# A gated mix of a 2-D spectral filter and a gated feed-forward: token pairs in the row layout, a sum of block products begun in PSUM, operand sums in place, half of the tiles by way of DRAM

## The chip, the cores and the metric

The kernel runs on one core of a Trainium2 chip. The metric is the device time of one execution in microseconds (us). A profiled execution of the kernel before gives the trace that is read here; three more give the times.

## The reference

Two branches are computed from the same x (2048 tokens by 576 features, float32) and mixed with a gate for each token:

```python
def _A_ref(x, w_r, w_i):
    X = jnp.fft.rfft2(x, axes=(-2, -1))
    X = X * (w_r + 1j * w_i)
    return jnp.fft.irfft2(X, s=(S, D), axes=(-2, -1))

def _B_ref(x, w_gate, w_up, w_down):
    g = jnp.einsum("bsd,df->bsf", x, w_gate)
    u = jnp.einsum("bsd,df->bsf", x, w_up)
    return jnp.einsum("bsf,fd->bsd", _gelu(g) * u, w_down)

g = _sigmoid((x * gate_w).sum(-1, keepdims=True))
return g * a + (1 - g) * b
```

The hidden size of the feed-forward is 4608, so branch B is three large matrix products; branch A is a Fourier transform over tokens and features, a product with a filter, and the way back.

## The kernel before

**The feed-forward** fills TensorE (PE). Each float32 operand is split into a high and a low part, so that a product of 128x512 takes three matmuls (high·high, high·low, low·high) plus tails. `PLAN` lists 36 steps in order: `"c"*2 + "s"*10 + "c"*11 + "s"*13`, the first half of the tokens in the first 18 and the second half in the others. A `c` step (`conv`) computes its products plainly. An `s` step (`products`) computes a 2x2 block product with seven products in place of eight: a11, a12, s2, s1, s3, s4, a22, numbered n = 0 to 6, each in two halves s = 0 and 1 of seven matmuls (`seven`, L1041 to L1044). The `s` operands (s1 to s4 and the splits of a11, a12, a22, in the tiles sx, gu2, xhi, xlo) are made once for each half of the tokens by `operands(p)`, from blocks that `load_xs` brings into xraw, tmp and misc. After each block, `down` multiplies the hidden tiles hb and hx with w_down (L835, pieces of twelve matmuls of 288 columns); ScalarE (ACT) scales the result into stg (L860), and GpSimd (POOL) adds it to yd in DRAM.

**PSUM** holds three pairs of banks that matter here: pgu, pone and pdn. In an `s` step the result of n = 0 stands in the banks of one pair and n = 1 in the other. ACT copies the first into gl (L214, `gl<-pgu` or `gl<-pone`), VectorE (DVE) adds the second to it (L1077), and `finish` takes gelu (L1068, ACT), the product with the other half (L1062, DVE), the rounding to the high part (L214, `hb<-gl`) and the low part (L1065, DVE). n = 2, 3, 4, 5, 6 go on in the same banks and in xraw.

**The spectral branch** (`spectral`) runs beside this on DVE and ACT, with some matmuls in `columns`. Its row transform of 576 points works on a tile `rows` of 128 x 5120 in which eight tokens are interleaved: element k of token t stands at 8k + t. It goes by a stage of nine (`forward_rows`) and radix-4 stages of width 8, 32 and 128 (`stage`, `_butterfly` L87) with `small_twiddles` (L444) and `large_twiddles` (L456). `into_tiles` and `into_rows` move between `rows` and `til`, in which each token has 290 elements in a row, with `moved` (L500): an ACT copy and a DVE product with a sign (L507) for each token, 289 elements at a time. `gate_sum` (L683) sums x·gate_w for a token. `columns` is the transform over tokens.

**The order.** Every engine takes its instructions in the order of the program, and the program's order is written by the kernel itself: PE pieces call `gap()` (L656), which pulls work from the generator `spectral` as long as `credit` is positive. Each PE piece adds its length to the credit (`tick`), each yielded DVE operation takes its own off, and the credit is cut at 1.2 us (L663). `at(n, …)` puts work n gaps later, and `seq`/`due` issue the steps of a hidden tile. `starts` are the two first steps of the runs of `s` (PLAN places 2 and 23); there the list `downs`, which says how many down pieces follow each of the seven products, differs from the other steps, because fewer hidden tiles are waiting.

## Time and profile before

| what | value |
|---|---|
| median of three runs | 1376.58 us (1374.06, 1376.58, 1377.76) |
| the profiled execution | 1374.25 us |
| its span, first to last instruction | 1372.5 us |
| mean granted clock of TensorE | 0.958 of full speed |
| DMA | 227.42 MB, 166 GB/s in the mean |

The span is what the trace covers; the execution's own time is 1.75 us longer. In the tables a line is given as `L1077`, then the engine, the operation, and `out<-in` by the names of the program. An idle time is put down to the instruction or DMA that released the engine last. A matmul's entry lasts longer than its spacing, because matmuls are pipelined: the next one starts before the entry of the last ends.

### The profile page before, as it was taken

The page shows a single profiled execution, that of the slowest core. Times are in us where ns is not written, and L with a number is a line of the kernel's source. Part 1 is how long each engine was busy: PE and PEld are TensorE (multiplying, and loading weights), DVE is VectorE, ACT ScalarE, POOL GpSimd, SP SyncE. Part 2 cuts the span into 40 slices and gives each one's busy share as a digit, 9 for nine tenths or more (in the row PEclk, how much of TensorE's full clock was granted, in tenths as well). Part 3 has the DMA queues.
Part 4 walks back from the last instruction along what each step waited for, and adds up shares of the span by engine and source line. Part 5 has one row for each costly group of instructions (what it writes and reads, how often), then busy time and mean ns, then how long its engine had stood idle before and what let it go on. Part 6 is the DMA issues. An engine that isn't in the chain of part 4 may idle for free.

```text
span 1372.5 us, 20070 instructions
## 1 busy us (share of the span) xinstructions
PE 1344.1 (98%) x7364; PEld 1186.9 (86%) x7364; DVE 1142.8 (83%) x1605; ACT 846.9 (62%) x1444; POOL 263.2 (19%) x322
## 2 busy tenths in 40 slices
PE   9998999999999999999999999889999999999998
PEld 7887888888889888889888988767888888888888
DVE  7689999989999768867786587689989779989854
ACT  5585676666674455465665544676676776676682
POOL 0011122221122222122210111211222232222231
PEclk9999999999999999999999999989999999999999
DMA  9465776696667877799987657744666797667797
GB/s 332 163 128 146 148 142 131 130 272 129 126 110 147 195 139 148 181 236 236 265 233 222 132 109 206 173 98 103 130 132 129 134 266 131 135 116 137 138 220 181
DMA packets 102770, 227.42 MB, mean 166 GB/s; under 512 B 12432, under 2 KB 22672, under 8 KB 101776
## 3 DMA queue, kind: packets, MB, share of 16 engines
q0 software_dynamic: 44928, 90.98, 44.1%
q1 hardware_dynamic: 57744, 135.17, 29.7%
q8 instruction: 57, 0.93, 0.3%
q14 instruction: 41, 0.34, 0.1%
HBM read 121.70 MB, written 97.26 MB: 160 GB/s over the span
## 4 chain that ended last, share of the span: by engine, by line
PE 85%; DVE 6%; ACT 4%; DMA 2%; issue 2%; SPq 0%; DVEq 0%; ACTq 0%
PE pdn L835 30%; PE pgu L1041 5%; PE pgu L1043 5%; PE pgu L1042 5%; PE pone L1041 5%; PE pgu L760 5%; PE pgu L762 5%; PE pgu L761 4%; PE pone L1043 4%; PE pone L1042 4%; PE pgu L1044 2%; PE pone L1044 2%; PE pone L760 2%; PE pone L762 2%; PE pone L761 2%
## 5 line engine op out<-in xcount | busy, mean ns | idle before, releaser
L848 POOL DMA_DIRECT2D yd<-stg x264 | 228.9, 868 | 994.2 <-ACT stg L860 861.2
L860 ACT ACTIVATE stg<-pdn,omg 128x576 f32<-128x576 f32 x276 | 203.9, 739 | 278.7 <-PE pdn L835 274.1
L835 PE MATMUL pdn<-dn,hb 128*128 128x288 f32 x2556 | 371.2, 295 | 2.5 <-DVE hb L1065 1.3
L835 PEld LDWEIGHTS pdn<-dn,hb 128*128 128x128 f32 x2556 | 357.8, 189 | 14.3 <-DVE hb L1065 1.8
L214 ACT ACTIVATE gu<-wq 64x256 fp32r<-64x256 f32 (+4 forms) x353 | 228.5, 666 | 101.7 <-DVE gu L1006 90.9
L1006 DVE TENSOR_TENSOR gu<-wq,gu 128x768 fp32r<-128x768 f32 x161 | 153.5, 953 | 18.9 <-ACT gu L214 18.5
L835 PE MATMUL pdn<-dn,hx 128*128 128x288 f32 x876 | 134.2, 295 | 0.2 <-DVE wq L899 0.2
L835 PEld LDWEIGHTS pdn<-dn,hx 128*128 128x128 f32 x876 | 124.9, 189 | 4.1 <-DVE wq L899 0.5
L760 PE MATMUL pgu<-xhi,gu 128*128 128x512 f32 x300 | 117.9, 393 | 0.0
L762 PE MATMUL pgu<-xlo,gu 128*128 128x512 f32 x300 | 117.8, 393 | 0.0
L761 PE MATMUL pgu<-xhi,gu 128*128 128x512 f32 x300 | 117.7, 392 | 0.0
L1023 DVE TENSOR_TENSOR wq<-wq 128x768 f32<-128x768 f32 x92 | 87.7, 953 | 7.9 <-ACT gu L214 7.9
L214 ACT ACTIVATE hb<-gl 128x512 fp32r<-128x512 f32 x66 | 41.4, 627 | 51.4 <-DVE gl L817 51.4
L762 PEld LDWEIGHTS pgu<-xlo,gu 128*128 128x128 f32 x300 | 56.6, 189 | 12.3
L760 PEld LDWEIGHTS pgu<-xhi,gu 128*128 128x128 f32 x300 | 56.8, 189 | 9.9
L761 PEld LDWEIGHTS pgu<-xhi,gu 128*128 128x128 f32 x300 | 56.7, 189 | 9.9
L1044 PE MATMUL pgu<-sx,gu 128*128 128x512 f32 x138 | 54.5, 395 | 6.6 <-ACT sx L214 6.6
L739 DVE TENSOR_TENSOR dn<-wq,dn 128x576 fp32r<-128x576 f32 x72 | 54.2, 753 | 5.0 <-ACT dn L214 5.0
L1041 PE MATMUL pgu<-xhi,gu 128*128 128x512 f32 x140 | 55.6, 397 | 2.5 <-DVE xraw L1077 2.4
L1041 PE MATMUL pgu<-sx,gu 128*128 128x512 f32 x140 | 55.7, 398 | 1.9 <-ACT gl L214 1.9
L1041 PE MATMUL pone<-xhi,gu 128*128 128x512 f32 x136 | 53.5, 394 | 3.7 <-DVE xraw L1077 3.7
L1043 PE MATMUL pgu<-sx,gu 128*128 128x512 f32 x140 | 55.2, 395 | 0.0
(243 smaller groups left out, 2871.2 us busy)
## 6 DMA issues: line engine op xcount, KB each, us to landing
yd<-stg POOLq DMA_DIRECT2D x264, 288.0 KB, 4.9
wq<-ws SPq DMA_DIRECT2D x92, 384.0 KB, 4.2
wq<-wd SPq DMA_DIRECT2D x72, 288.0 KB, 4.6
wq<-wgu SPq DMA_DIRECT2D x24, 640.0 KB, 5.8
colm<-col POOLq DMA_DIRECT2D x32, 256.0 KB, 6.3
tmp<-wf SPq DMA_DIRECT2D x16, 290.0 KB, 5.1
hx<-til SPq DMA_DIRECT2D x64, 72.5 KB, 5.0
til<-hx SPq DMA_DIRECT2D x64, 72.5 KB, 3.7
```

The costliest lines, as they stand in the source:

```text
L214: act.activation(o, i, AF.Copy)
L760: pe.matmul(ps, w[:, 0, k, c], xhi[tb][:, k], start=k == 0, stop=False)
L761: pe.matmul(ps, w[:, 1, k, c], xhi[tb][:, k], start=False, stop=False)
L762: pe.matmul(ps, w[:, 0, k, c], xlo[tb][:, k], start=False, stop=False)
L835: pe.matmul(ps[half], h[:, l, c], d[:, k, half * HD:(half + 1) * HD], start=part == 0 and n == 0, stop=part == 1 and n == 2)
L848: pl.dma_start(yd[u], o, accum_op=ALU.add)
L860: put(u, lambda o: act.activation(o.rearrange("p (c k) -> p c k", c=2), v[:, :, 0:HD], AF.Copy, scale=omg[:, u:u + 1]), i == 0)
L1006: vec.tensor_tensor(o, x.rearrange("p (c k) -> p c k", c=3), f(w[:, 256:1024]).rearrange("p (c k) -> p c k", c=3), ALU.subtract)
L1041: pe.matmul(ps, hi, xh[:, t], start=start and t == 0, stop=False, skip_group_check=True)
L1042: pe.matmul(ps, lo, xh[:, t], start=False, stop=False, skip_group_check=True)
L1043: pe.matmul(ps, hi, xl[:, t], start=False, stop=False, skip_group_check=True)
L1044: pe.matmul(ps, tl, xt, start=False, stop=stop, skip_group_check=True)
```

## The change

Five things are done together.

1. **Token pairs.** `rows` interleaves two tokens where it interleaved eight, in four groups. The radix-4 stages have the widths 2, 8 and 32, the small twiddles work on runs of 2, `moved` handles a pair of tokens in one instruction, and gates and output rows read every second element. The copies to and from the layout of `xn` follow (its load is now two DMAs).
2. **The first sum in PSUM.** In an `s` step ACT copies the result of n = 0 not into gl but into the other pair of banks (`copy(ps[1][s], v)`), and n = 1 accumulates onto it. The two DVE additions into gl go; gelu reads the bank (L1232 after) and so does the product (L1167 after). n = 1 now has to wait for the copy. `downs` changes in both forms.
3. **Operand sums in place.** `operands` forms s1 to s4 in the loaded blocks, with all three parts loaded earlier, its ACT copies handed out two at a step, and only s4 left for the last `c` step. The second set is loaded right behind `columns`.
4. **Half the tiles through DRAM.** The second eight tokens' tiles go to `bw` straight from `til`, and `fetched_rows` reads them back in pieces; before, they were moved into `rows` first and went to DRAM in that form. `fw` is written and read in quarters.
5. **Placing.** The credit is cut at 2.0 us in `columns` (`COLCAP`); the reload of x for the second half goes at other gaps; the weight slots (`early`, `where`) of the last `s` step before a `c` follow its place.

```diff
+COLCAP = 2.0
...
+        bw = dram.tile([P, 8 * SW], F32, name="bw", tag="bw")
...
+        def token_rows(rows, t):
+            return rows.rearrange("p (c g k t) -> p g t c k", c=2, g=4, t=2)[:, t // 2, t % 2]
...
-            v = rows.rearrange("p (b d e t) -> p b d e t", d=4, e=4, t=8)
-            tmps = [tmp[:, 320 * i:320 * (i + 1)].rearrange("p (b t) -> p b t", t=8) for i in range(4)]
-            tmps = [(x, x[:, 0:20], x[:, 20:40]) for x in tmps]
+            v = rows.rearrange("p (b d e t) -> p b d e t", d=4, e=4, t=2)
+            tmps = [tmp[:, 320 * i:320 * (i + 1)].rearrange("p (b t) -> p b t", t=2) for i in range(4)]
+            tmps = [(x, x[:, 0:80], x[:, 80:160]) for x in tmps]
...
+            yield from stage(rows, 2, TAKEN, -1)
+            yield from small_twiddles(rows, TAKEN, -1)
             yield from stage(rows, 8, TAKEN, -1)
-            yield from small_twiddles(rows, TAKEN, -1)
+            yield from large_twiddles(rows, TAKEN, -1)
             yield from stage(rows, 32, TAKEN, -1)
-            yield from large_twiddles(rows, TAKEN, -1)
-            yield from stage(rows, 128, TAKEN, -1)
...
         def moved(at):
 
+            s2 = sgn[:, None, :].to_broadcast([P, 2, KF])
             yield None
-            for t in range(8):
+            for g in range(4):
                 for c in range(2):
-                    o, i = at(t, c)
+                    o, i = at(slice(2 * g, 2 * g + 2), g, c)
                     if c:
-                        vec.tensor_tensor(o, i, sgn, ALU.mult)
-                        yield 0.66
+                        vec.tensor_tensor(o, i, s2, ALU.mult)
+                        yield 0.69
                     else:
                         copy(o, i)
-                yield None
+                if g % 2:
+                    yield None
...
+        def fetched_rows():
+
+            rows = rows_tile()
+            R = row_view(rows)
+            pl.memset(rows.rearrange("p (c k) -> p c k", c=8)[:, :, 2 * KF:], 0.0)
+            s2 = sgn[:, None, :].to_broadcast([P, 2, KF])
+            for b in range(2):
+                for i, x in enumerate(spots_of[b]):
+                    g, c = divmod(i, 2)
+                    o, x = R[:, 2 * b + g, c, :, 0:KF], x[:, :, 0:KF]
+                    if c:
+                        vec.tensor_tensor(o, x, s2, ALU.mult)
+                        yield 0.69
+                    else:
+                        copy(o, x)
+                if b == 0:
+                    yield None
+                    fetch(1)
+                    for _ in range(5):
+                        yield None
+            box[0] = rows
...
+            yield from beside(first_tiles(1))
             yield from into_tiles(0, rows)
             yield from first_tiles(0)
             cols[0] = True
             yield from columns()
             cols[0] = False
+            load_xs(1)
             yield from last_tiles()
-            load_xs(1, 0)
-            load_xs(1, 1)
-            yield from into_rows(1)
-            nc.sync.dma_start(bw, box[0])
             yield None
+            for i in range(4):
+                c = slice(2 * SW * i, 2 * SW * (i + 1))
+                nc.sync.dma_start(bw[:, c], til[0][:, 8 * SW:][:, c])
+                yield None
             yield from into_rows(0)
             yield from operands(1)
             yield from until(3)
+            fetch(0)
             yield from inverse_rows(0)
-            box[0] = rows_tile()
-            nc.sync.dma_start(box[0], bw)
-            for _ in range(5):
-                yield None
+            yield from fetched_rows()
             yield from inverse_rows(1)
...
+            credit[0] = min(credit[0], COLCAP if cols[0] else 1.2)
...
+            def sums(i):
+                a11, a12, a21, a22 = parts_of[i]
+                for o, x, z, op in ((a22, a21, a22, ALU.add), (a21, a11, a21, ALU.subtract),
+                                    (a11, a22, a11, ALU.subtract), (a12, a12, a11, ALU.subtract)):
                     vec.tensor_tensor(o, x, z, op)
-                    yield 0.72
-                sums = (("s1", m), ("s2", a11), ("s3", a21), ("s4", a12))
-                yield None
-                if i == 2:
-                    yield from tails_of([(ops[n][2], x) for n, x in sums])
-                else:
-                    for n, x in sums:
-                        copy(ops[n][0][:, i], x)
+                    yield 0.61
...
+                for n in raw:
+                    high(n, 2)
+                yield from sums(0)
+                for n in most:
+                    high(n, 0)
+                yield from sums(1)
+                for n in raw:
+                    low(n, 2)
+                    quarter(n)
+                    yield 0.61
+                for n in most:
+                    high(n, 1)
+                for n in most:
+                    low(n, 0)
+                    yield 0.61
+                while acts:
                     yield None
+                yield from sums(2)
+                for n in most:
+                    high(n, 2)
+                for n in most:
+                    low(n, 1)
+                    yield 0.61
+                while acts or current[0] < starts[p] - 1:
                     yield None
-                    for n, x in sums:
-                        vec.tensor_tensor(ops[n][1][:, i], x, f(ops[n][0][:, i]), ALU.subtract)
-                        yield 0.61
-                if i == 0:
-                    load_xs(p, 2)
+                for i in range(3):
+                    high("s4", i)
+                for n in most:
+                    low(n, 2)
+                    quarter(n)
+                    yield 0.61
+                while acts:
+                    yield None
...
+                if name == "c11":
+                    seq((name, q), (1, mult), (2, lambda: copy(h[:, 0], g)), (4, low))
+                elif done:
...
-            downs = (1, 1, 1, 1, 0, 0, 0) if q in starts else (0, 1, 1, 1, 2, 1, 2)
-            ps = {}
+            downs = (0, 0, 1, 0, 1, 1, 1) if q in starts else (1, 1, 1, 1, 1, 1, 2)
...
+                if n == 0:
+                    ps = {k: [banks[k]() for _ in range(2)] for k in range(2)}
+                elif n == 3:
...
-                    seven(v, q, n, name, s, n in (0, 1, 3), n in (1, 5, 6))
-                    if n in (0, 2, 3):
-                        copy({0: c1, 2: c2, 3: c3}[n][s], v)
-                    elif n in (1, 4, 5):
-                        o = {1: c1, 4: c3, 5: c2}[n][s]
+                    seven(v, q, n, name, s, n in (0, 3), n in (1, 5, 6))
+                    if n == 0:
+                        copy(ps[1][s], v)
+                    elif n == 1 and s == 0:
+                        act.activation(gl[0], v, AF.Gelu_apprx_tanh)
+                    elif n in (2, 3):
+                        copy({2: c2, 3: c3}[n][s], v)
+                    elif n in (4, 5):
+                        o = {4: c3, 5: c2}[n][s]
```

The line numbers of the kernel after differ: L214 (copy) is L218 there, L817 and L821 (`c`: product with the other half, low part) are L888 and L892, L1006 (low part of weights) L1111, L1023 (sums of weight blocks) L1128, L860 L931, L1068 L1173, L1062 L1167, L1065 L1170, L1077 L1184.

The order on ACT at the start of the second run of `s` steps (PLAN place 23). Before (sx: operand sums; hb: hidden tile of the last `c` step; gu: weights; the copies out of pgu are those of n = 0):

```order
L214 ACTIVATE sx_7678<-xraw_84 32x512 [waits DVE_49]
L214 ACTIVATE sx_7678<-xraw_84 32x512
L214 ACTIVATE sx_7678<-xraw_84 32x512 [waits DVE_49]
L214 ACTIVATE sx_7678<-xraw_84 32x512
L214 ACTIVATE gu1_71<-wq_77 128x768 [waits PE_49]
L214 ACTIVATE gu1_71<-wq_77 128x768
L214 ACTIVATE gl0_82<-pgu_7857 128x512 [waits PE_49]
L214 ACTIVATE gl1_83<-pgu_7858 128x512 [waits PE_49,Activation_49]
```

After, at the same place:

```order
L218 ACTIVATE hb0_78<-gl1_83 128x512 [waits DVE_49]
L218 ACTIVATE gu1_71<-wq_77 128x768 [waits DVE_49,PE_49]
L218 ACTIVATE gu1_71<-wq_77 128x768
L218 ACTIVATE pone_7807<-pgu_7805 128x512 [waits PE_49]
L218 ACTIVATE pone_7808<-pgu_7806 128x512 [waits PE_49]
L218 ACTIVATE gu1_71<-wq_77 64x256 [waits DVE_49]
L1232 ACTIVATE gl0_82<-pone_7807 128x512 [waits PE_49]
```

The operand copies are gone from this place (they stand further up), and the copies of n = 0 go into pone, behind a hidden tile and two weight copies, of which the first waits for DVE.

DVE at the same place. Before (the rows with sx and gu2 are the low parts of the operands):

```order
L1023 TENSOR_TENSOR wq_77<-wq_77 128x768 [waits DMAHW0_49,Activation_49]
L1023 TENSOR_TENSOR wq_77<-wq_77 128x768 [waits DMAHW1_49,DVE_49]
L817 TENSOR_TENSOR gl1_83<-gl1_83,pgu_7793 128x512 [waits PE_49]
L821 TENSOR_TENSOR hb0_78<-gl1_83,hb0_78 128x512 [waits Activation_49]
L974 TENSOR_TENSOR sx_7678<-orow_96,sx_7678 128x512 [waits Activation_49]
L974 TENSOR_TENSOR sx_7678<-tmp_89,sx_7678 128x512 [waits Activation_49]
L974 TENSOR_TENSOR sx_7678<-misc_95,sx_7678 128x512 [waits Activation_49]
```

After:

```order
L888 TENSOR_TENSOR gl1_83<-gl1_83,pgu_7785 128x512 [waits PE_49]
L892 TENSOR_TENSOR hb0_78<-gl1_83,hb0_78 128x512 [waits Activation_49]
L1128 TENSOR_TENSOR wq_77<-wq_77 128x768 [waits DMAHW7_49]
L1128 TENSOR_TENSOR wq_77<-wq_77 128x768 [waits DMAHW0_49,DVE_49]
L1111 TENSOR_TENSOR gu1_71<-wq_77,gu1_71 128x3x256 [waits Activation_49]
```

Here the operand work is gone, and the two sums of weight blocks stand behind the low part of the hidden tile, where they stood ahead of it.

ACT in an ordinary `s` step, the third of the second run. Before:

```order
L214 ACTIVATE hb0_78<-xraw_84 128x512 [waits DVE_49]
L214 ACTIVATE gu0_70<-wq_77 128x768
L214 ACTIVATE gl0_82<-pgu_8392 128x512 [waits PE_49]
L214 ACTIVATE gu0_70<-wq_77 64x256 [waits DVE_49]
L214 ACTIVATE gl1_83<-pgu_8393 128x512 [waits PE_49]
```

After:

```order
L218 ACTIVATE hb0_78<-xraw_84 128x512 [waits DVE_49]
L218 ACTIVATE gu0_70<-wq_77 128x768
L218 ACTIVATE pone_8345<-pgu_8343 128x512 [waits PE_49,Activation_49]
L218 ACTIVATE gu0_70<-wq_77 64x256 [waits DVE_49]
L218 ACTIVATE pone_8346<-pgu_8344 128x512 [waits PE_49]
```

The copies keep their places in the queue; their target is now the bank onto which n = 1 accumulates.

More of the change, by code (lines that the diff above doesn't have):

```diff
@@ L612, in spectral, with beside @@
             rows = rows_tile()
-            nc.sync.dma_start(rows, fw)
-            yield from first_tiles(1)
+            later_rows = rows
+            def beside(work):
+                q = quarters(lambda c: nc.sync.dma_start(later_rows[:, c], fw[:, c]))
+                n = 0
+                for v in work:
+                    yield v
+                    n += 1
+                    if n % 3 == 0:
+                        next(q, None)
+                for _ in q:
+                    yield None
+            yield from beside(first_tiles(1))
             yield from into_tiles(0, rows)
@@ L978, in operands @@
+            for v in steps():
+                for _ in range(2 if v is None else 1):
+                    if acts:
+                        acts.pop(0)()
+                yield v
             ops["done"] = p
@@ L1051, in products @@
             then = PLAN[q + 1] if q + 1 < len(PLAN) else None
-            c1, c2, c3 = gl, [xraw[:, k] for k in range(2)], [xraw[:, k] for k in range(2, 4)]
+            c2, c3 = [xraw[:, k] for k in range(2)], [xraw[:, k] for k in range(2, 4)]
             made = {}
```

190 lines of the change are left out of this document (112 added, 78 removed).

## The prediction

> **What bounds the kernel now.** First the page: the busy shares and the chain that ended last.
>
> ```profile
> span 1372.5 us, 20070 instructions
> PE 1344.1 (98%) x7364; PEld 1186.9 (86%) x7364; DVE 1142.8 (83%) x1605; ACT 846.9 (62%) x1444; POOL 263.2 (19%) x322
> PE 85%; DVE 6%; ACT 4%; DMA 2%; issue 2%; SPq 0%; DVEq 0%; ACTq 0%
> ```
>
> PE is busy for 98% of the span. The change neither adds nor removes a matmul, so what can be won is only the time in which PE waits. Second, the view of what PE waited for (us in total, times, longest):
>
> ```profile
> PE pgu L1044 <- ACT sx L214: 6.6, 1, 6.6
> PE pone L1041 <- DVE xraw L1077: 3.7, 2, 2.6
> PE pone L276 <- DVE colm L269: 2.8, 1, 2.8
> PE pgu L1041 <- DVE xraw L1077: 2.4, 2, 1.6
> PE pgu L1041 <- ACT gl L214: 1.9, 1, 1.9
> PE pdn L835 <- DVE hb L1065: 1.3, 2, 0.7
> PE pdn L835 <- ACT stg L860: 1.1, 1, 1.1
> ```
>
> Third, busy time by stretches, to see where these waits lie (columns: stretch, then PE, PEld, DVE, ACT, POOL busy with counts, granted clock, DMA share, GB/s):
>
> ```profile
> 100.00:125.00 25.00, 20.91 (x95) 16.46 (x95) 23.44 (x38) 15.24 (x28) 2.07 (x3) 0.95 0.41 108
> 160.00:500.00 340.00, 340.00 (x1893) 302.38 (x1892) 312.36 (x419) 207.65 (x364) 69.19 (x82) 0.95 0.75 156
> 690.00:710.00 20.00, 17.15 (x84) 14.62 (x84) 18.20 (x31) 12.04 (x21) 4.51 (x6) 0.87 1.02 254
> 885.00:945.00 60.00, 47.90 (x221) 38.97 (x220) 53.56 (x68) 41.70 (x73) 5.10 (x6) 0.87 0.38 86
> 703.60:707.00 3.40, 3.40 (x10) 2.66 (x9) 3.20 (x7) 2.09 (x5) 0.44 (x1) 0.50 1.07 276
> 891.30:898.10 6.80, 3.10 (x7) 2.48 (x8) 6.23 (x10) 6.57 (x13) 0.00 (x0) 0.50 0.00 0
> 908.40:911.80 3.40, 3.40 (x10) 2.62 (x10) 3.40 (x5) 1.03 (x2) 0.87 (x1) 0.50 0.52 55
> ```
>
> PE is full from 160 to 500 with DVE at 312.36 of 340: DVE is close behind, but it does not hold PE up there. The idle time lies in three places: 25.00 − 20.91 = 4.1 us just after the first run of `s` steps starts, 20.00 − 17.15 = 2.85 us in `columns`, and 60.00 − 47.90 = 12.1 us at the start of the second run. Behind these stalls stand stretches at half clock, in which work takes twice its time: half of 3.4, of the 3.1 busy, and of 3.4 is 1.7 + 1.55 + 1.7 = 4.95 us. An entry also outlasts its spacing (0.39 against 0.227 us, rows of 967 below), so each of about seven gaps is 0.16 us longer than it looks: 1.2 us. Together **25.2 us**, and a kernel with none of these would take 1374.25 − 25.2 = 1349.05 by the profiled execution's own time.
>
> Fourth, the timeline of ACT in the 6.6 us wait:
>
> ```profile
> 893.68 2.56 ACT L214 ACTIVATE sx<-xraw 32x512 fp32r<-32x512 f32 x4
> ...
> 898.09 1.66 ACT L214 ACTIVATE sx<-xraw 128x512 fp32r<-128x512 f32 x3
> 899.65 1.25 ACT L214 ACTIVATE sx<-orow 32x512 fp32r<-32x512 f32 x2
> 900.92 3.84 ACT L214 ACTIVATE sx<-xraw 32x512 fp32r<-32x512 f32 x6
> 904.78 1.58 ACT L214 ACTIVATE gu<-wq 128x768 fp32r<-128x768 f32 x2
> ```
>
> ACT is still making the operands of the steps that have already begun, and the copies out of PSUM stand behind these. That is a lump of work in one place, not a lack of ACT: 62% busy overall.
>
> **The change, part by part.**
>
> *Operands.* The same splits and sums are made, but the order now has all except s4's ahead of the last `c` step; for the second run the blocks are loaded behind `columns`. In the new order nothing of them is left at the start of either run, whereas the rows above show ACT on them until 904.76. With the lump go all waits of the 100:125 and 885:945 stretches: 4.1 + 12.1 idle, 1.55 + 1.7 half clock, six gaps of 0.16: **−20.4 us**. The work itself moves beside `c` steps, where between 710 and 885 ACT and DVE have room; this cover I cost at nothing:
>
> ```profile
> 710.00:885.00 175.00, 175.00 (x976) 155.80 (x975) 120.42 (x171) 95.97 (x156) 28.36 (x37) 0.95 0.69 168
> ```
>
> DVE is busy for 120 of 175 there. Were the cover gone, the lump of some 18 copies of 0.6 us would stand again.
>
> *The first sum in PSUM.* The additions that go are these, with the price of an ACT copy beside them:
>
> ```profile
> L1077 DVE TENSOR_TENSOR gl<-gl,pone 128x512 f32<-128x512 f32 x24 | 16.0, 682 | 0.5 <-PE pone L1044 0.5
> L1077 DVE TENSOR_TENSOR gl<-gl,pgu 128x512 f32<-128x512 f32 x22 | 14.6, 682 | 1.2 <-PE pgu L1044 1.2
> L214 ACT ACTIVATE xraw<-pgu 128x512 f32<-128x512 f32 x46 | 25.6, 580 | 0.0
> ```
>
> DVE loses 46 additions, 30.6 us, two in each of the 23 steps; since it doesn't hold PE in ordinary steps, this is worth nothing by itself. The ACT copy stays, and its target, a bank, has no row; its cost is taken as that of the copy out of one, 0.58. New is the wait: n = 1 must wait for the copy, and the copy stands in ACT's queue behind hidden tiles and weights. An ordinary step of before shows how late it is:
>
> ```profile
> 967.43 0.40 PE L1041 MATMUL pgu<-xhi,gu 128*128 128x512 f32 x1
> 967.67 0.39 PE L1042 MATMUL pgu<-xhi,gu 128*128 128x512 f32 x1
> ...
> 970.40 0.39 PE L1044 MATMUL pgu<-sx,gu 128*128 128x512 f32 x1
> 970.63 0.39 PE L1041 MATMUL pone<-xhi,gu 128*128 128x512 f32 x1
> 969.81 0.59 ACT L214 ACTIVATE gl<-pgu 128x512 f32<-128x512 f32 x1
> ...
> 971.39 0.57 ACT L214 ACTIVATE gl<-pgu 128x512 f32<-128x512 f32 x1
> 964.25 0.95 PE L835 MATMUL pdn<-dn,hb 128*128 128x288 f32 x6
> 965.04 0.96 PE L835 MATMUL pdn<-dn,hx 128*128 128x288 f32 x6
> ```
>
> The second copy starts 971.39 − 970.40 = 0.99 us after the start of the last matmul it needs and ends at 971.96. With the new `downs`, one down piece stands between n = 0 and n = 1: twelve matmuls at 0.79 for six, 1.58 us. The half that needs this copy would start another seven matmuls (1.59) on, at 970.63 + 1.58 + 1.59 = 973.8. So 1.8 us are in hand. I take **+0.9** for all 21 ordinary steps: half of the single wait of before that names this copy (1.9, `ACT gl`). The ends are 0 and 21 steps at the 0.58 of the copy, 12.
>
> At the two starts no down piece stands between, and more stands ahead. By the new order at the second start: PE's last `c` matmul ends, DVE takes the product (0.69, the L817/L821 kind), ACT hb (0.63), DVE the low part (0.69) and two weight sums, ACT two weight copies, then the bank copy. With
>
> ```profile
> L1023 DVE TENSOR_TENSOR wq<-wq 128x768 f32<-128x768 f32 x92 | 87.7, 953 | 7.9 <-ACT gu L214 7.9
> L817 DVE TENSOR_TENSOR gl<-gl,pgu 128x512 f32<-128x512 f32 x38 | 26.0, 685 | 31.2 <-PE pgu L767 31.1
> ```
>
> (the sums pitch about 0.9 apart), and 1.58 for the two weight copies (row of 904.78), this is 0.2 + 0.69 + 0.63 + 0.69 + 1.8 + 1.5 + 0.6 = 6.1 us behind the last `c` matmul. PE has the 14 matmuls of n = 0 meanwhile, 3.2 us. **+2.9 us**; bounds 0, if DVE's sums pass earlier, and 5. A stall of that size can halve the clock: the trace has it after the waits of 2.8 (at 702) and 1.9, not after that of 2.6 (at 105). At even odds on 1.7: **+0.8**. At the first start the two sums stand ahead of the product and partly beside PE's work: 1.5 less, **+1.4**, no clock.
>
> A rule of the Trainium skill bears on the clock ("TensorE: Matmul & The Clock Gate", section on the HAM clock gate): a free-running window of about 3.4 us, and a drop after an idle window. The three waits, all under 3.4, agree with its free phase, not with a need for 3.4 us of idle; by that length the 0.8 would be 0.
>
> *Token pairs.* The moves and gates work on strided elements in before, on a stride of two after:
>
> ```profile
> L99 DVE TENSOR_TENSOR til<-til 128x290 f32<-128x290 f32 x32 | 13.3, 456 | 0.2
> L507 DVE TENSOR_TENSOR til<-rows,sgn 128x289 f32<-128x289 f32 x16 | 11.1, 719 | 0.0
> L507 DVE TENSOR_TENSOR rows<-til,sgn 128x289 f32<-128x289 f32 x16 | 10.5, 746 | 4.2 <-DMA bw<-rows 4.2
> L94 DVE TENSOR_TENSOR rows<-rows 128x1280 f32<-128x1280 f32 x36 | 53.5, 1487 | 0.2
> ```
>
> Stride 8 costs 719/456 = 1.58 times unit stride. A run or stride of two has no row: bounds are unit rate and 1.58 times. I take unit rate, since the three stage widths of before (8, 32, 128) share the one mean of 1487, so that runs of 8 don't cost. Then 32 moves of 0.73 become 16 of about 0.76, 11 us less on DVE, worth nothing to PE. The Trainium skill ("Advanced Engine Details and Errata", SBUF Cachelines) says that two hits in a 16-byte line absorb the latency; two adjacent floats, or two at stride two, are such a pair. By that it is unit rate too; stride 8 at 1.58 agrees.
>
> *Half the tiles through DRAM* takes 8 moves off the time between `columns` and the second run; its DMAs wait behind nothing that PE needs. 0, with −1 to +2 for landings that come late.
>
> *Columns.* The 2.85 + 1.7 + 0.16 = 4.7 us there came when reloads of x met a column step. Gaps and cap both change, the collision may move: I take **+2.0** left, between 0 and 4.7 (above it, up to 8, if the cap of 2.0 brings work in larger bursts).
>
> Sum: 1349.05 + 0.9 + 2.9 + 0.8 + 1.4 + 2.0 = **1357.05**. The median of the runs is 2.3 above the profiled one, which I leave out: it is within their spread of 3.7.
>
> **The rivals.**
>
> *All stalls go.* ACT and DVE are early enough at both starts, nothing meets in `columns`: 1349, with a remnant 1350. For it: the queues are emptier than in any row of before. Against: the chain of 6.1 us at the second start stands in the order. 0.15.
>
> *A stall is left in `columns` or at a start that I don't see.* The lump moved beside `c` steps pushes a hidden tile or a column step late. Price 5 to 10 us, 1362 to 1367. For it: 885:945 shows how a few us of lateness multiply, by the clock and the next steps. 0.20.
>
> *Slower: the bank copies.* The copy takes the place of DVE as what PE waits for in each of the 21 ordinary steps. It decides where the copy comes later than the 1.8 us in hand by x: 21x, against 17 us won. Slower than before from x = 0.8; at 1.5, 1357 − 0.9 + 31 = 1388. For it: ACT's queue is in order, and hidden tile and weights before the copy wait for DVE. Against: at 967 the copy was 1.8 early, and DVE gets 30.6 us lighter. 0.06.
>
> *Slower or equal: runs of two cost 1.58 times.* A width-2 stage is 6 operations of 1.41 and 4 of 0.74 by the kernel's own costs, 11.4 us; four passes, 45.7, cost 0.58 more: 26.5, with twiddles of two perhaps 35. In stretches where DVE has only 340 − 312 = 28 of 340 free, minus its 30.6 lighter load, half would reach PE: 1357 + 18 = 1375. 0.04.
>
> *The change does not remove the lump*: the operands wait for late landings and pile up again: 1370 to 1374. 0.05.
>
> **How the numbers follow.** Forecast as worked out (1353 to 1361): 0.50. All stalls go 0.15, a stall unseen 0.20, lump 0.05, bank copies 0.06, runs of two 0.04. The range from 1348 to 1368 takes in the first three, 0.85, which with the spread of the runs I count as 0.8. A measurement of this kernel can tell about 0.3%, 4 us, from no change: faster by more is below 1372.4, the first three and half of the lump, 0.87; within, the other half and runs of two, 0.07; slower, 0.06.
>
> **What would show it.** Right: no PE wait on `ACT sx` or `DVE xraw` at the starts; ACT's sx copies end before the second run; a wait of 2 to 4 us of pone on the copy at its start, and smaller ones on the first; 46 additions into gl missing; width-2 operations at 1.49 us like the others. Wrong: waits of n = 1 on the copy in most steps, entries of 128x1280 above 2 us in width 2, or a PE wait in `columns` above 5 us.

## The result

| | median us | runs | profiled execution | its span |
|---|---|---|---|---|
| before | 1375.92 | 5, 1374.06 to 1377.76 | 1374.25 | 1372.5 |
| after | 1368.31 | 5, 1366.67 to 1370.01 | 1368.03 | 1366.1 |

The ratio is 0.9947, with a 95% interval of 0.9932 to 0.9962: faster by 7.6 us, 0.5%. The forecast was 1357 (range 1348 to 1368), 17.2 us below the profiled execution of before, 19.6 below the median then on record.

### The profile page after: what moved, and what is told of

Its sections match the earlier page's. It is cut to its first block, busy times and chain, and to the rows that moved or that the text cites. A ratio compares the mean times of both kernels' runs of the same rounds, so it can differ in the third digit from the quotient of the medians.

```text
span 1366.1 us, 19980 instructions
## 1 busy us (share of the span) xinstructions
PE 1344.1 (98%) x7364; PEld 1185.5 (87%) x7364; DVE 1104.2 (81%) x1543; ACT 833.0 (61%) x1428; POOL 264.5 (19%) x323
## 4 chain that ended last, share of the span: by engine, by line
PE 79%; DMA 8%; DVE 7%; ACT 3%; issue 2%; SPq 1%; DVEq 0%; ACTq 0%
PE pdn L906 27%; PE pgu L1146 5%; PE pone L1146 5%; PE pgu L1148 5%; PE pgu L1147 5%; PE pone L1148 5%; PE pone L1147 5%; PE pgu L831 3%; PE pgu L833 3%; PE pgu L832 3%; DMA hx<-til 3%; PE pgu L1149 2%; PE pone L1149 2%; PE pone L831 2%; PE pone L833 2%
## 5 line engine op out<-in xcount | busy, mean ns | idle before, releaser
L906 PE MATMUL pdn<-dn,hb 128*128 128x288 f32 x2508 | 364.9, 295 | 1.4 <-DVE dn L810 1.0
L906 PEld LDWEIGHTS pdn<-dn,hb 128*128 128x128 f32 x2508 | 352.3, 188 | 13.9 <-DVE dn L810 1.2
L931 ACT ACTIVATE stg<-pdn,omg 128x576 f32<-128x576 f32 x276 | 204.0, 740 | 246.3 <-PE pdn L906 241.8
L218 ACT ACTIVATE gu<-wq 64x256 fp32r<-64x256 f32 (+4 forms) x353 | 230.1, 666 | 92.2 <-DVE gu L1111 58.7
L1111 DVE TENSOR_TENSOR gu<-wq,gu 128x768 fp32r<-128x768 f32 x161 | 153.6, 955 | 39.9 <-ACT gu L218 37.1
L906 PE MATMUL pdn<-dn,hx 128*128 128x288 f32 x924 | 142.9, 295 | 0.5 <-DVE wq L970 0.2
L906 PEld LDWEIGHTS pdn<-dn,hx 128*128 128x128 f32 x924 | 132.1, 188 | 4.9 <-DVE wq L970 0.5
L831 PE MATMUL pgu<-xhi,gu 128*128 128x512 f32 x296 | 115.9, 392 | 1.2 <-DVE gl L888 1.2
L832 PE MATMUL pgu<-xhi,gu 128*128 128x512 f32 x296 | 115.6, 390 | 0.0
L1128 DVE TENSOR_TENSOR wq<-wq 128x768 f32<-128x768 f32 x92 | 87.5, 953 | 5.0 <-ACT gu L218 4.8
L218 ACT ACTIVATE hb<-gl 128x512 fp32r<-128x512 f32 x68 | 42.7, 628 | 55.5 <-DVE gl L888 53.3
L888 DVE TENSOR_TENSOR gl<-gl,pgu 128x512 f32<-128x512 f32 x37 | 25.3, 684 | 42.5 <-PE pgu L838 42.3
L1146 PE MATMUL pgu<-xhi,gu 128*128 128x512 f32 x140 | 55.6, 397 | 2.6 <-ACT pgu L218 2.6
L1146 PE MATMUL pgu<-sx,gu 128*128 128x512 f32 x140 | 55.0, 393 | 1.7 <-DVE gl L1167 1.7
L1147 PE MATMUL pgu<-xhi,gu 128*128 128x512 f32 x140 | 55.2, 394 | 0.0
```

What stands on the lines that cost most here:

```text
L218: act.activation(o, i, AF.Copy)
L831: pe.matmul(ps, w[:, 0, k, c], xhi[tb][:, k], start=k == 0, stop=False)
L832: pe.matmul(ps, w[:, 1, k, c], xhi[tb][:, k], start=False, stop=False)
L906: pe.matmul(ps[half], h[:, l, c], d[:, k, half * HD:(half + 1) * HD], start=part == 0 and n == 0, stop=part == 1 and n == 2)
L931: put(u, lambda o: act.activation(o.rearrange("p (c k) -> p c k", c=2), v[:, :, 0:HD], AF.Copy, scale=omg[:, u:u + 1]), i == 0)
L1111: vec.tensor_tensor(o, x.rearrange("p (c k) -> p c k", c=3), f(w[:, 256:1024]).rearrange("p (c k) -> p c k", c=3), ALU.subtract)
```

## The profile after

The page's first lines:

```profile
span 1366.1 us, 19980 instructions
PE 1344.1 (98%) x7364; PEld 1185.5 (87%) x7364; DVE 1104.2 (81%) x1543; ACT 833.0 (61%) x1428; POOL 264.5 (19%) x323
PE 79%; DMA 8%; DVE 7%; ACT 3%; issue 2%; SPq 1%; DVEq 0%; ACTq 0%
```

The third line gives each engine's share of the chain of work that ended last. PE's busy time is what it was; DVE has lost 38.6 us. What PE waited for (us in total, times, longest):

```profile
PE pone L1146 <- ACT pone L218: 3.0, 1, 3.0
PE pgu L1146 <- ACT pgu L218: 2.6, 1, 2.6
PE pone L831 <- ACT gl L878: 2.3, 1, 2.3
PE pgu L1146 <- DVE gl L1167: 1.7, 1, 1.7
PE pgu L1322 <- DVE gate L1318: 1.5, 1, 1.5
PE pgu L831 <- DVE gl L888: 1.2, 1, 1.2
PE pone L283 <- ACT til L218: 1.1, 1, 1.1
PE pdn L906 <- DVE dn L810: 1.0, 1, 1.0
```

No wait names sx or xraw any more. At the top stand two waits on the bank copies (L218), each once, one at each start. The 2.3 belongs to the first `c` step, and the 1.7 is a wait on the product that now reads a bank (L1167). The stretches of before, and two at half clock (columns as in the prediction: stretch, then PE, PEld, DVE, ACT, POOL busy with counts, granted clock, DMA share, GB/s):

```profile
100.00:125.00 25.00, 25.00 (x137) 21.96 (x135) 23.35 (x39) 14.70 (x27) 3.46 (x4) 1.00 0.63 131
160.00:500.00 340.00, 337.26 (x1867) 298.33 (x1867) 300.95 (x397) 208.13 (x363) 69.40 (x82) 1.00 0.74 153
690.00:710.00 20.00, 18.81 (x108) 16.28 (x106) 14.30 (x25) 13.62 (x24) 2.89 (x4) 1.00 1.02 259
885.00:945.00 60.00, 56.99 (x293) 49.16 (x292) 49.53 (x57) 35.87 (x64) 8.26 (x10) 0.97 0.61 126
87.30:90.70 3.40, 3.40 (x9) 2.62 (x9) 3.37 (x5) 0.92 (x3) 0.00 (x0) 0.50 0.00 0
899.70:903.10 3.40, 3.40 (x10) 2.64 (x9) 3.40 (x4) 1.14 (x4) 0.00 (x0) 0.50 0.00 0
```

The second start lost 12.1 us of PE time before and loses 3.0 now, but 160:500, where PE was full, now has 2.7 us of idle time, and both starts are followed by 3.4 us at half clock. (The wait of the first start stands before 100 now, at 84.)

To compare all kernels place by place, the excess of each matmul's spacing over its steady value (0.227 us for 512 columns, 0.1315 for 288, 0.135 for 290) is added up over the same pieces of the program: the begin, up to about the first `s` step; the first two `s` steps of each run ("start"); what lies between the first start and the columns; the stretch in which `columns` runs; and the rest. The steady sum is 1323.9 us in every kernel. Figures in us, from one profile each; the begin alone, in kernels whose order is the same up to there, lies between 6.0 and 8.5, so a difference of a us or two in one column of one profile says little:

| kernel | begin | 1st start | s steps, c | columns | 2nd start | from there on | all |
|---|---|---|---|---|---|---|---|
| before | 6.3 | 5.9 | 1.8 | 6.2 | 17.2 | 4.1 | 42.3 |
| after | 8.3 | 5.0 | 5.8 | 7.2 | 5.2 | 3.9 | 36.1 |
| e1_sum_in_sbuf | 6.4 | 2.9 | 1.8 | 7.2 | 2.1 | 11.8 | 33.1 |
| e2_operands_alone | 8.1 | 3.0 | 1.8 | 6.0 | 12.5 | 4.1 | 36.2 |
| e3_sum_in_psum_alone | 8.2 | 8.6 | 11.9 | 9.0 | 16.8 | 4.4 | 59.7 |
| e4_down_at_starts | 8.0 | 1.7 | 5.3 | 5.7 | 2.0 | 5.3 | 28.8 |
| e5_later_rows | 8.1 | 4.9 | 2.2 | 5.3 | 6.3 | 6.0 | 33.6 |
| e6_colcap | 6.9 | 4.9 | 7.4 | 2.5 | 5.2 | 4.0 | 31.7 |
| e7_starts_mended | 6.1 | 1.4 | 2.2 | 4.6 | 0.3 | 5.7 | 21.1 |
| e8_sum_in_sbuf_rate | 6.2 | 3.2 | 1.8 | 7.9 | 3.6 | 2.7 | 26.2 |
| e9_old_operands | 8.6 | 9.2 | 5.3 | 7.0 | 9.2 | 2.8 | 45.2 |
| e10_later_fetch | 7.7 | 1.2 | 2.2 | 8.2 | 0.3 | 4.6 | 25.0 |
| e11_old_reload | 6.2 | 3.3 | 10.2 | 4.5 | 6.5 | 5.2 | 36.6 |
| e12_all_mends | 8.0 | 1.7 | 2.2 | 7.8 | 0.3 | 4.5 | 25.4 |
| e13_later_copy | 6.0 | 1.4 | 2.2 | 6.2 | 0.3 | 4.4 | 21.4 |
| e14_later_copy_alone | 8.5 | 2.3 | 5.7 | 6.0 | 3.6 | 5.3 | 32.4 |

(Two short pieces between these places, under 1 us together but for 3.1 in e9, are in the last column alone.)

## The experiments

Times are medians; ratios are to before, with the 95% interval.

### Parts alone and parts undone

**e1_sum_in_sbuf**: `products` of before in the kernel after.

```diff
...
-                    if n == 0:
-                        copy(ps[1][s], v)
...
+                    if n in (0, 2, 3):
+                        copy({0: c1, 2: c2, 3: c3}[n][s], v)
...
```

> The kernel after, with the first sum back in gl: ACT copies n = 0 into gl, DVE adds n = 1 (46 additions, 30.6 us of DVE more), downs as before; everything else of the change stays. Theory A (the bank copies at the two starts are what ate the gain: 2.8 and 3.2 us of wait there, each with a half clock of 3.4 us behind, 1.6 us lost): both waits go, 1368.3 - 9 = 1359 us (1356 to 1362). Rival B (the starts are late because of the weight sums and hidden tiles on DVE and ACT, whoever reads the bank; DVE, 30.6 us heavier, then waits elsewhere): 1366 to 1371 us, with PE waits of over 2 us still at both starts.

1364.12 us, 0.9923 (0.9899 to 0.9946). Against after (0.9932 to 0.9962) the intervals overlap, so the times alone don't decide; the trace does. Both waits on the copies are gone (1st start 5.0 to 2.9, 2nd 5.2 to 2.1), and so is the 1.7 on L1167, as theory A has it. But near the end stands something that neither theory had. ACT's timeline of this kernel:

```profile
1303.77 1.63 ACT L581 ACTIVATE tmp<-rows,gs 128x640 f32<-128x640 f32 x2
1309.42 0.86 ACT L581 ACTIVATE tmp<-rows,gs 128x640 f32<-128x640 f32 x1 [4.03 <-DMA yd<-tmp]
1311.66 0.87 ACT L581 ACTIVATE tmp<-rows,gs 128x640 f32<-128x640 f32 x1 [1.38 <-DMA yd<-tmp]
1313.10 0.86 ACT L581 ACTIVATE tmp<-rows,gs 128x640 f32<-128x640 f32 x1 [0.57 <-DMA yd<-tmp]
1313.86 0.83 ACT L218 ACTIVATE gu<-wq 128x768 fp32r<-128x768 f32 x1
1314.59 1.07 ACT L218 ACTIVATE gl<-pgu 128x512 f32<-128x512 f32 x2
```

The spectral work wasn't done when the last step came. The kernel then issues all that is left without a matmul between (`while gens: gap()`). The output rows wait for each other's transfers, and the copy of n = 0 stands behind them: PE waited 6.1 us, with 6.8 us at half clock behind it. So the 46 additions are not free to have: they take credit.

**e8_sum_in_sbuf_rate** gives that credit back.

```diff
-RATE = 1.0
+RATE = 1.02
```

> The kernel after with the first sum back in gl (as in the run e1_sum_in_sbuf) and the rate of the schedule's credit at 1.02 in place of 1.0, so that the spectral work is issued before the last step and not in one lump there. Theory A (the first sum in PSUM buys no time of DVE that counts, only credit; without its wait and without the lump of 6.2 us of wait and a half clock at the end, all is won): 1364.1 - 9 = 1355 us (1353 to 1359). Rival B (DVE, 30.6 us heavier and driven faster, falls behind in the s steps and PE waits there in small pieces): 1362 to 1370 us.

1357.82 us, 0.9877 (0.9862 to 0.9892): inside theory A's range, 3 us above its estimate. The lump at the end is gone (11.8 to 2.7), but 2nd start and columns are 1.5 and 0.7 us worse. Without the first sum in PSUM, the other parts and 2% of rate are some 17 us faster than before. The kernel after with this rate was not run, so how much of the 10 us below after is the rate's stays open.

**e2_operands_alone**: before, with the new `operands` and its loads.

```diff
...
-            yield from last_tiles()
-            load_xs(1, 0)
-            load_xs(1, 1)
+            load_xs(1)
+            yield from last_tiles()
...
```

> The kernel before with the operand sums in place and the earlier loads alone (part 3). Theory A (the operand lump alone made the stalls at both starts: 12.1 us idle and 3.3 of half clock at the second, 4.1 at the first): 1376 - 16 = 1360 us (1357 to 1364), the columns stall of 4.4 us stays. Rival B (operands are late for want of DVE time that only the rest of the change frees): 1368 to 1376 us, with waits on operands still there.

1368.19 us, 0.9949 (0.9929 to 0.9969): rival B. ACT at the second start of this kernel:

```profile
893.01 1.28 ACT L214 ACTIVATE sx<-orow 32x512 fp32r<-32x512 f32 x2 [0.81 <-DVE sx L959]
894.29 2.55 ACT L214 ACTIVATE sx<-tmp 32x512 fp32r<-32x512 f32 x4
896.86 1.27 ACT L214 ACTIVATE gu<-tmp 32x512 fp32r<-32x512 f32 x2
898.14 1.58 ACT L214 ACTIVATE gu<-wq 128x768 fp32r<-128x768 f32 x2
899.63 1.06 ACT L214 ACTIVATE gl<-pgu 128x512 f32<-128x512 f32 x2
```

The operands are still being made when the step begins; only the wait has another name (`ACT gl`, 4.3 us). In the program's order the loop that finishes the operands ahead of a start issues, at the second start, 45 instructions in one piece before, 32 here, 31 in e3, 17 in e9, and none in the kernel after. At the first start it issues 19 before, and 6 here and in the kernel after.

**e9_old_operands**: the complement, after with the `operands` and late loads of before. (In it the sums x·gate_w of the first eight tokens read an operand block in place of gate_w; the instructions are the same.)

```diff
-            for i in (2, 1):
-                load_part(0, i)
...
+            load_xs(1, 0)
+            load_xs(1, 1)
...
```

> The kernel after with the operand sums of the kernel before (part 3 undone, loads late again). In the order of this kernel no operand work is left in a lump at the second start, though it is at the first. Theory A (what removed the lump at the second start is the room that the other parts make in the schedule, fewer moves ahead and more credit, not the new operand sums): second start as in the profile after, within 2 us, first start 2 to 5 us worse: 1370 to 1374 us. Rival B (the new operand sums removed it, as the prediction had it): the wait on sx of some 6 us is back at the second start, 1380 us or more.

1377.17 us, 1.0019 (1.0008 to 1.0029): by the letter neither theory, in substance rival B. No wait on sx is back, but the prices are near B's:

```profile
PE pgu L1109 <- ACT pgu L218: 6.1, 1, 6.1
PE pone L1109 <- ACT pone L218: 6.0, 1, 6.0
```

In the program's order the old operands end just before the starts; in time ACT is on them until 906.3 at the second start, 7.3 us after the first matmul of the step (899.0), and the bank copy behind them passes the lateness on to PE. So the new operands are worth some 9 us here and 7 in the kernel before. They and the rest need each other: without the rest the lump stays, without them the bank copies cost 12 us of wait and 6.8 us at half clock twice. Parts 1, 4 and 5 were never run by themselves.

**e3_sum_in_psum_alone**: before, with `products` of after.

```diff
...
-                    if n in (0, 2, 3):
-                        copy({0: c1, 2: c2, 3: c3}[n][s], v)
...
+                    if n == 0:
+                        copy(ps[1][s], v)
...
```

> The kernel before with the first sum in PSUM alone (part 2, with its downs). Theory A (the copy is a new wait for PE behind ACT's queue, and at the starts that queue is full of operands): slower, 1377 to 1385 us, waits on the bank copy at both starts. Rival B (DVE, 30.6 us lighter, gets rid of part of the lump): 1368 to 1373 us.

1389.5 us, 1.0094 (1.0061 to 1.0127): theory A's direction, above its range. Its PE waits, and below them DVE's longest in the s steps (timeline):

```profile
PE pone L1041 <- ACT pone L214: 8.9, 1, 8.9
PE pgu L1041 <- ACT pgu L214: 7.1, 3, 6.1
PE pdn L835 <- DVE hx L1065: 3.8, 1, 3.8
```

```profile
294.56 0.96 DVE L1023 TENSOR_TENSOR wq<-wq 128x768 f32<-128x768 f32 x1 [12.11 <-DMA wq<-ws]
```

The 8.9 and 6.1 are the copies behind operands. The 3.8 is another story. With DVE's credit freed, the spectral work reaches the load of its second half some 7 us earlier (282.7 against 290.0). That transfer now goes out just ahead of the weights on the same queue, DVE stands 12.1 us for weights, and PE waits for a hidden tile. Of the 17 us by which its profile's excess is above that of before, 10 stand in that place (column "s steps, c").

### Mending the new waits

**e4_down_at_starts**

```diff
-            downs = (0, 0, 1, 0, 1, 1, 1) if q in starts else (1, 1, 1, 1, 1, 1, 2)
+            downs = (1, 0, 1, 0, 0, 1, 1) if q in starts else (1, 1, 1, 1, 1, 1, 2)
```

> The kernel after with one down piece (12 matmuls, 1.58 us) moved to between n = 0 and n = 1 at the two starts: downs (1,0,1,0,0,1,1). Theory A (PE waits there for the bank copy alone): each wait shrinks by 1.6, to 1.2 and 1.6 us, and no half clock follows: 1368.3 - 6 = 1362 us (1361 to 1366). Rival B (the down piece itself waits for the hidden tile of the step before, so the wait only changes its name): 1367 to 1369 us.

1361.72 us, 0.9902 (0.9878 to 0.9925): theory A, to 0.3 us. 1st start 5.0 to 1.7, 2nd 5.2 to 2.0, no half clock at either. A wait of 1.6 was left at the second.

**e5_later_rows**

```diff
-            for _ in range(6):
+            for _ in range(10):
                 yield None
             yield from forward_rows(1, rows)
```

In the timeline of DVE after, the cause of the 1.7 on L1167:

```profile
300.35 0.69 DVE L437 TENSOR_TENSOR tmp<-rows 128x512 f32<-128x512 f32 x1 [6.91 <-DMA rows<-xn]
...
307.08 0.68 DVE L1167 TENSOR_TENSOR gl<-gl,pgu 128x512 f32<-128x512 f32 x1
```

> The kernel after with the first DVE work on the second half of x put off by 10 places of the schedule behind its load, not 6. In the profile after, DVE stood 6.9 us before that work until the load landed, and PE then waited 1.9 us for the late product that holds a PSUM bank. Theory A (the load is what was late, the bank's reader passes the lateness on): that DVE wait is under 2 us, the 1.9 us wait of PE goes, 1366 us (1365 to 1368). Rival B (DVE is simply behind in these steps): PE's wait stays, 1368 us.

1364.51 us, 0.9921 (0.9907 to 0.9936). DVE's wait for the load fell from 6.9 to 1.9 us and PE's wait at that place went (s steps 5.8 to 2.2): theory A. The median is 1.5 us below its estimate and not clear of after's. A wait of 2.2 on the same product came up elsewhere, at 1113 us, behind DVE's waits of 5.0 and 2.9 for the pieces fetched from bw.

**e7_starts_mended**: e4, e5, and at the starts the first bank copy ahead of the two weight copies, the second ahead of one.

```diff
-                    prep_b(q, 2, -1)
+                    prep_b(q, 2, 1)
...
-                prep_b(q + m // 7, m % 7, (0, 1, 0, 0, 0, 0, 2)[n])
+                prep_b(q + m // 7, m % 7, (2 if q in starts else 0, 1, 0, 0, 0, 0, 2)[n])
```

> The kernel after with three mends: a down piece between n = 0 and n = 1 at the two starts, at these starts the first bank copy ahead of the two weight copies and the second ahead of one, and the load of the second half given 10 places. Theory A (the bank copies stood behind weight copies, and the load was late): no PE wait above 1 us at either start, 1361.7 - 3.5 = 1358 us (1355 to 1360). Rival B (weights that now come later are waited for instead): 1361 to 1364 us with waits of PE on the weight copies.

1354.87 us, 0.9853 (0.9838 to 0.9868): 13 us below after and 21 below before. Its longest waits:

```profile
PE pgu L1322 <- DVE gate L1318: 1.5, 1, 1.5
PE pone L1146 <- DVE gl L1167: 1.4, 1, 1.4
PE pone L283 <- DVE colm L276: 1.3, 2, 1.2
```

The second start is down to 0.3 us. The 1.4 on L1167 (at 1101 us) is the one that e5 had at 1113, and e4 at 1109: DVE stands 5.4 and 2.2 us for the pieces fetched from bw. In after DVE stood 4.7 and 1.5 us there, and PE did not wait.

**e10_later_fetch**: e7 with 10 places for that fetch.

```diff
                     fetch(1)
-                    for _ in range(5):
+                    for _ in range(10):
```

> The kernel of the run e7_starts_mended with 10 places of the schedule, not 5, between the second fetch from bw and its first use. There DVE stood 5.4 and 2.2 us for the landing, and PE then waited 1.5 us for the product that holds a PSUM bank. Theory A (a late transfer holds DVE, and the bank's reader behind it holds PE): the 1.5 us go, 1354.9 - 1.9 = 1353 us (1351 to 1355). Rival B (the wait moves on to the next hidden tile): 1354 to 1356 us.

1354.56 us, 0.9862 (0.984 to 0.9885): no change to be seen, inside both theories' ranges. The wait on L1167 went, 5.7 to 4.6 at that place, but begin and columns of this execution were 1.6 and 3.6 us worse.

### Columns

**e6_colcap**

```diff
-COLCAP = 2.0
+COLCAP = 1.2
```

> The kernel after with the credit cut at 1.2 us in columns too, not 2.0. Theory A (larger bursts of spectral work in columns make the four waits of 1.1 to 1.3 us there): these waits, 4.8 us, shrink by half or more: 1366 us (1364 to 1367). Rival B (they come from reloads of x and from DMA hops that a column step waits for, whatever the cap): still 4 to 6 us in columns, 1367 to 1370 us, more if the spectral work then ends late.

1363.94 us, 0.9925 (0.9908 to 0.9941): columns 7.2 to 2.5, theory A, though 1.6 came back in the s steps.

**e11_old_reload**: the kernel of e6 with `reload_x` and `load_x` of before.

> The kernel after with the reload of x at the gaps and in the order of before, and the credit cut at 1.2 us in columns. Theory A (the new placing is what makes columns no better): the four small waits go back to one of about 3 us with a half clock, as before: 1368 us (1366 to 1370) with 4.4 us in one place. Rival B (placing does help, and without it more is lost): 1370 to 1374 us.

1368.11 us, 0.9956 (0.9941 to 0.9971). The time fits A, the places don't: columns 4.5, and the s steps, whose order this edit leaves alone, at 10.2 against 5.8. There the load of x's second half, issued at the same place, landed after 15.7 us (13.1 in after); DVE stood 9.6 us for it, and PE 4.6 with 6.8 us at half clock behind.

**e12_all_mends**: e10 with the cap at 1.2.

> The kernel of the run e10_later_fetch with the credit cut at 1.2 us in columns. Theory A (each of the mends removes its own stall and they add): columns fall from 8.2 to about 2.5 us of excess, 1354.6 - 5 = 1350 us (1348 to 1352), about 25 us or 1.8% below before. Rival B (with the smaller cap the spectral work ends later, and loads and hidden tiles that were just early enough are late again, as at 304 us in the run e6_colcap): 1352 to 1356 us.

1354.52 us, 0.9849 (0.9836 to 0.9863): no gain over e10, rival B's range. But what B named is not what came: the s steps stayed at 2.2, and columns at 7.8, 5.4 of it in three waits of one kind, 16 us apart:

```profile
PE pone L283 <- DVE colm L276: 4.9, 3, 2.1
```

**e14_later_copy_alone** and **e13_later_copy**: after, and e12, with one copy in `columns` a place later.

```diff
                     elif g == 1:
-                        if kb + 1 < 16:
-                            copy(xh2, two(Z[kb + 1]))
                         corner(kb - 2, 2, True)
                     elif g == 2:
+                        if kb + 1 < 16:
+                            copy(xh2, two(Z[kb + 1]))
```

> The kernel after with one edit in columns: the ACT copy of the next column block (xh2) one place later, behind the hop of its corners through DRAM. In the profiles ACT stands for that hop's landing (2.4 to 4.2 us), and the copies behind it (parts of x, hidden tiles) make DVE and then PE late. Theory A (the late hop at the head of ACT's queue makes the columns waits): columns' excess falls from 7.2 to under 4 us: 1365 us (1363 to 1367). Rival B (what is late is the DVE work between that copy and the product, which now comes even later): 1368 to 1371 us, columns 7 us or more.

> The kernel of the run e12_all_mends with the same edit in columns, the copy of the next block one place later. Theory A (the hop's landing at the head of ACT's queue): columns' excess falls from 7.8 to under 4 us: 1350 us (1348 to 1352). Rival B (the DVE work behind the copy is what is late): 1354 to 1358 us.

1364.82 us, 0.9928 (0.9904 to 0.9951), and 1354.11, 0.9852 (0.983 to 0.9875). ACT's wait for the hop in this stretch halved (17.2 to 7.8 us, and 15.2 to 8.3), PE's excess fell only from 7.2 to 6.0 and from 7.8 to 6.2. e14's time is theory A's, but by luck: 2.7 and 1.6 us of it came at the two starts, which this edit leaves alone. The hop is at most a part of it, not the cause. What sets columns between 2.5 and 8.2 us stays open: cap, reload and hop each moved it in one kernel and not in another, and every kernel meets the reload at another phase.

## Why the prediction was wrong

By the profiled executions, 1357.05 was forecast and 1368.03 came: 11.0 too little. Two things of the prediction failed in their mechanism: at the first start the operands were not gone (term 1), and it had no term for the reader that now holds the bank (term 4). Of the rest, columns were mis-sized and the begin is chance. Term by term (wait with the 0.16 of each gap, half clock at 1.6):

1. **First start**, forecast 1.4 without half clock; 2.8 + 1.6 = 4.4. **+3.0.** The step that failed is "In the new order nothing of them is left at the start of either run", and with it that the two weight sums pass "partly beside PE's work". The loop that finishes the operands still issues 6 instructions just ahead of this start. PE's first matmul of the step began at 81.12; DVE's low parts of operands ran until 81.97 and ACT's copies of operands until 84.14. So the two sums began only at 81.90, and the product L888, which stands behind them, at 83.76, when n = 0 was nearly done. ACT, DVE, DVE, ACT, in the timeline after:

```profile
82.89 1.25 ACT L218 ACTIVATE gu<-tmp 32x512 fp32r<-32x512 f32 x2
81.90 1.94 DVE L1128 TENSOR_TENSOR wq<-wq 128x768 f32<-128x768 f32 x2
83.76 0.68 DVE L888 TENSOR_TENSOR gl<-gl,pgu 128x512 f32<-128x512 f32 x1
86.47 1.06 ACT L218 ACTIVATE pgu<-pone 128x512 f32<-128x512 f32 x2
```

(gu in the first row is the tile gu2, s4.) A wait forecast too short for a half clock got one. With the old operands, 19 instructions here, this start costs 9.2 (e9). No run takes the 6 away alone, so how much of the 2.8 is theirs, and how much the order of sums and product, stays open.
2. **Second start**, 2.9 + 0.8 forecast; 3.2 + 1.6 = 4.8. **+1.1.** The mechanism and its size were right. DVE, then ACT, in the timeline after:

```profile
893.06 0.69 DVE L888 TENSOR_TENSOR gl<-gl,pgu 128x512 f32<-128x512 f32 x1 [2.33 <-PE pgu L838]
894.45 0.69 DVE L892 TENSOR_TENSOR hb<-gl,hb 128x512 fp32r<-128x512 f32 x1 [0.70 <-ACT hb L218]
895.05 1.94 DVE L1128 TENSOR_TENSOR wq<-wq 128x768 f32<-128x768 f32 x2
```

```profile
893.78 0.63 ACT L218 ACTIVATE hb<-gl 128x512 fp32r<-128x512 f32 x1 [2.57 <-DVE gl L888]
897.09 1.58 ACT L218 ACTIVATE gu<-wq 128x768 fp32r<-128x768 f32 x2 [2.68 <-DVE wq L1128]
898.57 1.06 ACT L218 ACTIVATE pone<-pgu 128x512 f32<-128x512 f32 x2
```

Product, hidden tile, low part, two sums, two weight copies, bank copy, in this order. e4, which gives PE a down piece meanwhile, left a wait of 1.6 of it, and e7, which also puts the copy ahead of the weights, left none.

3. **Columns**, 2.0 forecast; four waits of 1.1 to 1.3, 4.8. **+2.8.** "The collision may move" was right, and it moved into four places; the term of 2.0, near the middle of its bounds, was mis-sized, and 4.8 lies just above the upper one. Why stays open, as said above.
4. **s steps and the `c` steps behind them**, 0.9 forecast for the bank copies; 1.9 + 0.65 + 0.56 = 3.1. **+2.2**, and by another mechanism. None of the 42 copies in ordinary steps held PE: the 1.8 us in hand were enough, and the slower rival built on these copies fell. The 0.56 is a down piece at the first `c` step and has to do with neither. What held PE in the other two is the other end of the same edit: the bank of n = 1 is now free only when DVE has taken the product (L1167), so DVE's lateness reaches PE. At the 1.9 it came from a load given 6 places where before had 9; with 10 the wait there is gone (e5). The prediction gave this reader no term.
5. **The begin**, 0 forecast; 8.3 against 6.3. **+1.9**, and not the change's doing: in the kernels here whose order is the same up to there, it lies between 6.0 and 8.5, and e3, whose order up to there is that of before, has 8.2.

The sum's first line held as to the names: the waits on sx and xraw went. Its reason did not. At the second start it is true of all parts together that nothing of the operands is left, and it was booked to the operands alone; e2 shows that they alone leave 12.5 us there, and e9 that the rest without them gives everything back. "Worth nothing by itself", said of the 46 additions that go, was wrong both ways: the credit that they leave pulls a large load forward into the way of the weights (in e3, 10 of 17 us), and it brings the spectral work home in time (e1). All but the last of the prediction's signs of being right came, and the time did not: none of them looked at the terms that failed.

Token pairs were priced right:

```profile
L96 DVE TENSOR_TENSOR rows<-rows 128x1280 f32<-128x1280 f32 x36 | 53.9, 1498 | 0.3
L104 DVE TENSOR_TENSOR rows<-tmp,rows 128x1280 f32<-128x1280 f32 x24 | 36.3, 1511 | 0.2
L520 DVE TENSOR_TENSOR til<-rows,sgn 128x578 f32<-128x578 f32 x8 | 5.6, 754 | 0.0
```

A third of each stage group has width 2. The first group's mean rose from 1487 to 1498, the second's from 1490 to 1511, so a run of two takes about 1487 + 3·11 = 1520 and 1490 + 3·21 = 1553, 2 and 4% more, not 58%. The moves take 754 for 578 elements, as an operation on 580 elements in a row does (760, L102 of before): unit rate. That this is worth nothing to PE was not tested alone.

## What to carry to other kernels

When a copy becomes something that TensorE waits for, price the whole queue ahead of it at the places where a phase begins, and price the other end too: who frees the bank, and what can make that reader late. In a schedule that is paid by a budget, taking work away moves every later load and lump; measure each part alone before booking a gain to it. And after taking a large stall away, expect several small ones, each with its chance of a half clock.

## What the runs showed of the hardware

The same code with the same wait at the second start got a half clock in one execution and none in another: after (wait 3.0, clock 0.50 from 899.7) and e14 (wait 3.0, and the stretch behind it at full clock):

```profile
PE pone L1146 <- ACT pone L218: 3.0, 1, 3.0
```

```profile
895.30:898.70 3.40, 3.10 (x14) 2.55 (x15) 3.40 (x5) 1.87 (x5) 0.00 (x0) 1.00 0.00 1
```

In e5 and e11 the same wait of 3.0 came with 6.8 us at half clock (0.50 from 892.6 and from 896.5), and this start cost 6.3 and 6.5 us, against 5.2 in after and 3.6 in e14. So up to 2.9 us of such a place is chance. So is the landing of a large load: that of x's second half took 12.5 us in e14, 13.1 in after, 14.4 in e6 and 15.7 in e11, with the same order ahead of it, and PE's excess behind it was 1.8, 1.9, 2.9 and 4.6 us. A granted clock of 0.95, shown over most of before, against 1.00 after, is not seen in the matmuls: 0.227 us apart in both. And a copy by ACT from bank to bank takes what a copy out of a bank takes:

```profile
L218 ACT ACTIVATE pone<-pgu 128x512 f32<-128x512 f32 x24 | 13.7, 578 | 0.3
```
